# Bias stage without GpSimd work and with blocks in alternating halves, eight copies of remainder rows, an earlier k split and scatters in two places

## The chip, the cores and the metric

The kernel runs on one core of one Trainium2 chip. The metric is the device time of one execution in microseconds (us); lower is better. Engines are PE (TensorE), DVE (VectorE), ACT (ScalarE), POOL (GpSimd) and SP (SyncE, which here only issues DMAs). A name with a q at its end (SPq, POOLq) is the engine's instruction sequencer, and PEld is the load of weights into PE.

## The reference

Two layers in float32, attention and then a mixture of experts. Attention has 8 batches, 8 heads, 576 positions and 64 columns a head, and a bias that depends on the two positions alone and is made by a small MLP with 32 hidden units:

```python
pos = np.arange(S)
rel = (pos[:, None] - pos[None, :]).astype(np.float32)
x = (np.log1p(np.abs(rel)) / np.log1p(np.maximum(pos[:, None].astype(np.float32), 1.0)))[..., None]
bias = np.maximum(x @ w1 + b1, 0.0) @ w2
scores = scale * np.matmul(q, k.transpose(0, 1, 3, 2)) + bias.transpose(2, 0, 1)[None]
attn = softmax(scores)                      # rows less their maximum
y = np.matmul(attn, v)
```

The rows of y, one for each of the 4608 tokens with 512 columns, go to the experts. Each token takes the one expert of eight with the largest logit:

```python
logits = x @ w_gate + modality_bias[modality_id]
e_idx, gate_w = np.argmax(logits, axis=1), max of softmax(logits)
for e in range(E):
    mask = e_idx == e
    h = np.maximum(x[mask] @ w1[e], 0.0)            # 512 -> 1024
    out[mask] = gate_w[mask, None] * (h @ w2[e])    # 1024 -> 512
```

## The kernel before, in words

The program is one stream that Python writes in order; each engine runs its own instructions in that order, and waits where one depends on another engine or on a DMA. Nothing reorders it. There are four stages.

**Bias (0 to 75 us).** Every element of the bias is an MLP of log1p of the distance, so a hidden row is a shifted window of one table: `xTb[0]` holds the table scaled by w1 (loaded in two pieces from `c_tg`, scaled by L157), and one hidden instruction (L179, on DVE or ACT) adds a column and takes the maximum with 0 over 128 partitions (4 rows of the bias by 32 units) and 576 columns. Four of these make a block: `bias_out` (L182) multiplies them with w2 on PE, `bias_put` (L197) scales the PSUM result into one of four output buffers (in `xTb[1]`) on ACT, or on DVE for the blocks in PUT_DVE, and SP stores the output into the bias tables in SBUF. 32 blocks fill the main table `NBm`, of 128 partitions; each store writes 16 partitions, 8 heads and 576 columns. `bias_base` (L48) says which: block blk writes partitions o + 64 half and every fourth of 16 behind it, with c = blk % 4, half = blk // 4 % 2 and o = blk // 8, so that four blocks in a row write the same half of the partitions. Four further blocks, made in `bias_late` (L249) during the first pair of heads, fill `NBr`, the bias of the last 64 rows, with eight copies each (L212). ON_DVE names the blocks of which DVE makes all four hidden instructions; in the others ACT makes one.

Beside the blocks stand hooks by block (`first_steps`, L524): loads of q, k and v of the first two pairs, the split of q and k into a rounded part and the rest (`split`, L352: a cast at L356 and a subtraction at L357, both on POOL), their transposes (`prep`), and the steps of `route_setup` (L616), which makes the constants of routing (memsets, loads, the id table's fill, the modality bias `mbias` at L691) on POOL and SP, one step at each block of ROUTE.

**Attention (75 to 700 us).** There are 32 pairs of heads, four to a batch. For a pair, 576 query rows make five tiles, u = 0 to 4 (four of 128 rows, one with the remainder). ORDER (L559) is a string of letters for each u: S scores (`scores`, L406), e and f exponentials, C the compaction of remainder rows on POOL (L455), t and T transposes of the exponentials, R, a, A, b and c the product with v, 0 to 4 the transposes of q and k of pair n+1, W the swap of QT (`swap`, L391: two DMAs on SP that bring columns to the other half of the partitions), K the heads' copies, V and L loads, q the split of q of pair n+2, k the split of k of pair n+1. X, B, Z and D are routing of the batch before: X and B its arithmetic and its rows, D their store to `xg` in DRAM (L883, on SP), and Z one scatter of token ids into the expert table `tab` by an indirect DMA that POOL issues (L862). `route_next` (L887) takes the next step of a list when the list it needs has come far enough.

**First expert tiles (700 to 790 us).** `first_tiles` (L1223) puts into the last four pairs what the first tiles need: the ids, the first expert's w1 at (2, 0) and w2 at (3, 4), each a tuple of pair and u. The weights go into slots of `NBm` (`moe_early`, L898) whose bias rows are no longer needed. `tile` (L1192) works on 256 rows: `phase1` (L1144) multiplies with w1, `phase2` (L1165) with w2, where `wsplit` (L1115) splits weights into two parts by a cast on ACT (L1123, L1130) and a subtraction on DVE (L1124, L1131). For tile 0 three of w2's subtractions run on POOL. The last batch's routing runs beside tile 0 in steps (`moe_first`, L1249).

**The other tiles (790 to 1185 us)** run to the end by tables of the tokens an expert has.

## Time and profile before

| | us |
|---|---|
| median of three runs (1186.39 to 1190.75) | 1189.63 |
| the profiled execution | 1186.77 |
| its span in the trace | 1184.9 |
| PE busy in it | 1125.8 |
| DVE, ACT and POOL busy | 756.1, 727.6, 384.0 |

The mean granted clock of PE was 0.988. The span is the time from the first to the last instruction of the trace; the execution's own time is 1.9 us longer. A busy engine is one with an instruction in flight; for PE that counts matmuls that overlap. In rows of waits, `<-` inside a name separates output and inputs of an instruction, and in brackets stands how long it waited and what came last. A row by stretches has the stretch, its length, then busy us and instructions (of all engines in the order PE, PEld, DVE, ACT, POOL where five are given), the granted clock of PE as a share of full speed, the busy share of the 16 DMA engines and what they moved in GB/s.

### The profile page before, as it was taken

How to read it: one execution, taken by the hardware profiler on the slowest of the kernel's cores; microseconds unless marked ns; L12 is line 12 of the kernel's file. 1: busy time of each engine (PE TensorE's matmuls, PEld its weight loads, DVE VectorE, ACT ScalarE, POOL GpSimd, SP SyncE). 2: the span in 40 equal slices, each digit the busy share in tenths (PEclk: the TensorE clock that was granted, in tenths of full speed). 3: DMA queues.
4: the chain of work that ended last, by engine and by line, in shares of the span. 5: the costliest groups of instructions: out<-in, count | busy, mean ns of one | idle time of the engine just before them, and what ended most of it. 6: DMA issues, size and time to landing. Idle time of an engine off the chain costs nothing. (4 is left out here: it accounts for less than half of the span.)

```text
span 1184.9 us, 23097 instructions
## 1 busy us (share of the span) xinstructions
PE 1125.8 (95%) x8202; PEld 915.2 (77%) x8202; DVE 756.1 (64%) x1552; ACT 727.6 (61%) x1412; POOL 384.0 (32%) x525
## 2 busy tenths in 40 slices
PE   7976999999999999999999979999999999999997
PEld 3455777767778677777877757988999899999975
DVE  7974567556665575766757647677456645655567
ACT  5564667667777576677775745555455545544576
POOL 2303222534534434344353224622221222122121
PEclk9997999999999999999999989999999999999999
DMA  6954444564544545444454540221123314211371
GB/s 173 197 120 123 110 104 99 113 112 121 118 102 114 107 121 104 120 120 109 114 123 96 162 103 25 70 54 37 45 64 107 117 45 159 92 46 54 116 251 30
DMA packets 91312, 124.27 MB, mean 105 GB/s; under 512 B 35697, under 2 KB 60657, under 8 KB 91188
## 3 DMA queue, kind: packets, MB, share of 16 engines
q1 hardware_dynamic: 83188, 101.35, 34.9%
q0 software_dynamic: 8000, 21.35, 6.0%
q8 instruction: 68, 1.11, 0.5%
q14 instruction: 56, 0.46, 0.2%
HBM read 140.09 MB, written 19.90 MB: 135 GB/s over the span
## 5 line engine op out<-in xcount | busy, mean ns | idle before, releaser
L436 DVE CUSTOM_DVE_ANT_0 Eb<-sps,NBm 128x576 f32<-128x576 f32 x256 | 190.1, 755 | 175.3 <-PE sps L421 85.5
L450 ACT ACTIVATE Eb<-Eb,mn 128x576 f32<-128x576 f32 x288 | 221.3, 769 | 42.5 <-DVE mn L436 37.9
L421 PE MATMUL sps<-KT,QT 128*128 128x288 f32 x1152 | 221.2, 318 | 21.1 <-DMA QT<-QT 19.3
L421 PEld LDWEIGHTS sps<-KT,QT 128*128 128x128 f32 x1152 | 165.1, 190 | 26.7 <-issue 18.1
L1157 PE MATMUL p<-QT,w1hi 128*128 128x256 f32 x1152 | 163.8, 285 | 5.0 <-ACT w1hi L1130 5.0
L464 PE MATMUL eps<-idf,Eb 128*128 128x128 f32 x1024 | 158.0, 280 | 0.5 <-DVE lgs L784 0.3
L1157 PEld LDWEIGHTS p<-QT,w1hi 128*128 128x128 f32 x1152 | 150.7, 193 | 7.1 <-ACT w1hi L1130 5.9
L508 PE MATMUL xps<-eT,vraw 128*64 128x288 f32 x1024 | 153.5, 421 | 1.5 <-DVE QT L1142 1.0
L1183 POOL DMA_INDIRECT out<-mo,idt x36 | 51.9, 1440 | 290.6 <-ACT mo L1182 262.2
L464 PEld LDWEIGHTS eps<-idf,Eb 128*128 128x128 f32 x1024 | 113.6, 141 | 38.3 <-issue 28.2
L1160 DVE SCALAR_TENSOR_TENSOR hl<-p,hh 128x512 fp32r<-128x512 f32 x72 | 49.7, 690 | 138.2 <-ACT hh L1159 134.4
L455 POOL COPY rem<-Eb 128x128 f32<-128x128 f32 x128 | 37.7, 295 | 275.4 <-ACT Eb L450 268.8
L1174 PE MATMUL p<-w2lo,hh 128*128 128x512 f32 x288 | 112.9, 392 | 3.5 <-DVE w2lo L1124 2.2
L310 ACT ACTIVATE eT<-eps 128x512 f32<-128x512 f32 x192 | 111.1, 591 | 6.3 <-PE eps L464 5.5
L1124 DVE TENSOR_TENSOR w2lo<-NBm,w2hi 128x1024 fp32r<-128x1024 f32 x81 | 98.7, 1225 | 25.2 <-ACT w2hi L1123 23.6
L1174 PE MATMUL p<-w2hi,hh 128*128 128x512 f32 x288 | 114.0, 396 | 0.0
L1174 PE MATMUL p<-w2hi,hl 128*128 128x512 f32 x288 | 112.5, 391 | 0.0
L1159 ACT ACTIVATE hh<-p 128x512 fp32r<-128x512 f32 x72 | 43.0, 598 | 110.6 <-PE p L1157 101.2
L310 ACT ACTIVATE xTb<-xps 128x288 f32<-128x288 f32 x64 | 26.3, 412 | 121.5 <-PE xps L518 119.5
L1124 DVE TENSOR_TENSOR w1lo<-NBm,w1hi 128x1024 fp32r<-128x1024 f32 x84 | 97.9, 1228 | 0.0
L508 PEld LDWEIGHTS xps<-eT,vraw 128*64 128x64 f32 x1024 | 62.6, 137 | 45.7 <-issue 11.4
L1157 PE MATMUL p<-QT,w1lo 128*128 128x256 f32 x576 | 93.1, 284 | 1.0 <-DVE w1lo L1131 1.0
(227 smaller groups left out, 1991.8 us busy)
## 6 DMA issues: line engine op xcount, KB each, us to landing
NBm<-moe_w SPq DMA_DIRECT2D x24, 2048.0 KB
NBm<-moe_w SPq DMA_DIRECT2D x46, 1024.0 KB
QT<-QT SPq DMA_DIRECT2D x64, 304.0 KB
NBm<-xTb SPq DMA_DIRECT2D x32, 288.0 KB
KH<-KT SPq DMA_DIRECT2D x64, 144.0 KB
qraw<-q SPq DMA_DIRECT2D x32, 256.0 KB
kraw<-k SPq DMA_DIRECT2D x32, 256.0 KB
vraw<-v SPq DMA_DIRECT2D x32, 256.0 KB
```

Source lines behind the costliest of these rows:

```text
L310: self.nc.scalar.activation(out, ps, AF.Copy, scale=scale)
L421: nc.tensor.matmul(ps[:, half, :], q, k[:, HS * half : HS * half + HS], start=i == 0, stop=i == len(terms) - 1, skip_group_check=True,)
L436: nc.vector.tensor_tensor_reduce(out=e.rearrange("p (t w) -> p t w", t=2), in0=ps, in1=nb.rearrange("p (t w) -> p t w", t=2), scale=1.0, s ...
L450: self.nc.scalar.activation(e, e, AF.Exp, bias=mn, scale=-1.0, accum_out=sm)
L464: nc.tensor.transpose(ps[:, k, :], e[:, part, P * k : P * k + P], self.idf)
L508: nc.tensor.matmul(ps[o, :], v[:, h, k, :], self.eT[:, h, k, sl], start=k == 0, stop=False, tile_position=(0, 64 * h), skip_group_check=True,)
L1124: (lo or self.nc.vector).tensor_tensor(l, w, h.bitcast(F32), op=ALU.subtract)
L1157: nc.tensor.matmul(ps[:, a, :], w[:, c, fs], x[:, c, :], start=i == 0, stop=i == len(ops) - 1)
L1159: nc.scalar.activation(hh[:, sl, :], ps, AF.Relu)
L1160: nc.vector.scalar_tensor_tensor(hl[:, sl, :], ps, 0.0, hh[:, sl, :].bitcast(F32), op0=ALU.max, op1=ALU.subtract)
L1174: nc.tensor.matmul(ps, h[:, f, sl], m[:, f, :], start=i == 0, stop=i == len(ops) - 1)
L1183: nc.gpsimd.indirect_dma_start(out=self.out, out_offset=IndirectOffsetOnAxis(ap=ids, axis=0), in_=o, in_offset=None, bounds_check=self.n_t ...
```

## The change

The new code, part by part:

- **Blocks.** `bias_base` now takes half = blk % 2, c = blk // 2 % 4 and o = blk // 8, so that blocks in a row write different halves. The offsets of the table change with it: X0 is 115 instead of 131, and the remainder blocks have a table of their own, `tg1` (loaded at block 15, scaled by ACT at block 23), whose rows are ordered so that a block's 16 rows are neighbours. A remainder block is then stored by two copies of 16 partitions each instead of eight of 4.
- **Who does what in the bias stage.** ON_DVE has 5 blocks instead of 9, PUT_DVE 3 instead of 2. Two small loads go through ACT's queue. The splits of pairs 0 and 1 are a cast on ACT and, two blocks later, a subtraction on DVE (`early`). The load of v of pair 0 moves from block 0 to block 19.
- **Routing's set-up.** Its memsets move ahead of the bias stage, six loads stay beside the blocks (ROUTE), and the other loads, the fills of `tab` and `xg`, and the modality bias move to u-steps of pairs 1 to 3 (ROUTE_LATE), with `xrb` as their buffer.
- **ORDER.** k is split at u = 4 for pair n+2 instead of u = 0 for pair n+1. Z stands at u = 0 and u = 2 and no longer at u = 3; scatters have a list of their own, and what is left of it runs behind the last pair.
- **First expert tiles.** The slots of `NBm` are shared out differently (w1's and w2's first weights in slots 0 and 1), the load of w2 stands at (3, 0) instead of (3, 4), all of w2's subtractions are DVE's and stand ahead of the routing steps, `phase2` runs the products with the low part of w2 last, and routing's steps beside tile 0 come two later.

```diff
@@ -41,22 +41,22 @@
-X0 = 131
-TW = X0 + S4
+X0, X1 = 115, 15
+TW, TW1 = X0 + S4, X1 + S4
...
-        c, half, o = blk % 4, blk // 4 % 2, blk // 8
+        half, c, o = blk % 2, blk // 2 % 4, blk // 8
         return o + 16 * cg + 64 * half, c
-    return P + cg, blk - NMAIN
+    return P + 4 * (blk - NMAIN) + cg, 0
@@ -110,17 +112,20 @@
-    ON_POOL, ON_DVE = (), (1, 6, 11, 15, 17, 21, 24, 27, 29)
+    ON_POOL, ON_DVE = (), (1, 8, 15, 22, 29)
...
-    PUT_DVE, ON_ACT2 = (21, 34), ()
-    PREP0, SWAP0, HEADS0, QK1, SPLIT1 = (9, 10, 13, 14, 17), 20, 23, (9, 10, 11, 12, 13, 14), 17
-    ROUTE = (1, 1, 2, 4, 5, 6, 7, 8, 15, 16, 17, 20, 21, 24, 25, 26, 27, 28, 29, 29)
+    PUT_DVE, ON_ACT2 = (21, 31, 34), ()
+    SPLIT0, PREP0, SWAP0, HEADS0, QK1, SPLIT1 = (3, 5), (9, 10, 13, 14, 17), 20, 23, (9, 10, 11, 12, 13, 14), (18, 21)
+    V0, TG1 = 19, (15, 23)
+    ROUTE = (6, 7, 8, 15, 16, 18)
+
+    ROUTE_LATE = ((1, 1), (1, 2), (1, 3), (1, 4), (2, 0), (2, 1), (2, 3), (3, 0), (3, 1))
@@ -128,21 +133,23 @@
-        nc.sync.dma_start(wb[:, 0:1], io["w1"].rearrange("o m -> m o"))
         nc.sync.dma_start(cb, io["c_bias"])
-        nc.sync.dma_start(wb[:, 1:2], io["b1"].rearrange("(m o) -> m o", o=1))
+        nc.scalar.dma_start(wb[:, 0:1], io["w1"].rearrange("o m -> m o"))
         nc.sync.dma_start(wb[:, 2 : 2 + H], io["w2"])
+        nc.scalar.dma_start(wb[:, 1:2], io["b1"].rearrange("(m o) -> m o", o=1))
@@ -206,10 +213,9 @@
-            for cg in range(4):
-                for par in range(2):
-                    r0 = 64 * par + 4 * cg + c
-                    nc.sync.dma_start(self.NBr[r0 : r0 + 49 : 16, :, :], o[32 * cg + par : 32 * cg + 32 : 2, :])
+            r0 = 16 * (blk - NMAIN)
+            for par in range(2):
+                nc.sync.dma_start(self.NBr[64 * par + r0 : 64 * par + r0 + 16, :, :], o[par:P:2, :])
@@ -349,12 +354,16 @@
-    def split(self, n, part):
+    def split(self, n, part, early=False):
...
+        lo = lambda eng: eng.tensor_tensor(xs[:, :, 1, :], x, xs[:, :, 0, :].bitcast(F32), op=ALU.subtract)
+        if early:
+            self.nc.scalar.copy(xs[:, :, 0, :], x)
+            return lambda: lo(self.nc.vector)
         self.nc.gpsimd.tensor_copy(xs[:, :, 0, :], x)
-        self.nc.gpsimd.tensor_tensor(xs[:, :, 1, :], x, xs[:, :, 0, :].bitcast(F32), op=ALU.subtract)
+        lo(self.nc.gpsimd)
@@ -531,13 +540,19 @@
-        add(0, lambda: self.load_v(0))
-        add(2, lambda: self.split(0, 0))
-        add(4, lambda: self.split(0, 1))
+        add(self.V0, lambda: self.load_v(0))
+        for part in range(2):
+            early(self.SPLIT0[part], 0, part)
+        add(self.TG1[0], lambda: self.nc.sync.dma_start(self.tg1, self.io["c_tg1"]))
+        add(self.TG1[1], lambda: self.nc.scalar.activation(self.tg1, self.tg1, AF.Copy, scale=self.w1c[:, 0:1]))
@@ -556,17 +572,20 @@
-        "S R S e f k X T a t B C Z",
+        "S R S e f X T a t B C Z",
         "L D S 1 A t e S 4 f 0 C T",
         "t S W S e f b q C Z T",
-        "B S c e S T 3 2 t f C Z V",
-        "S K X X e T B X t D",
+        "B S c e S T 3 2 t f C V",
+        "S K k X X e T B X t D",
@@ -595,21 +614,25 @@
-                    elif op in "qL":
+                    elif op in "qkL":
                         if n + 2 < n_pair:
-                            self.split(n + 2, 0) if op == "q" else self.load_qk(n + 2)
+                            self.load_qk(n + 2) if op == "L" else self.split(n + 2, "qk".index(op))
...
+                    elif op == "Z":
+                        self.route_scatter()
...
+        while self.scatters:
+            self.route_scatter()
@@ -829,6 +855,8 @@
+            if b < self.B - 1:
+                self.scatters += [s_scatter(c) for c in range(5)]
@@ -883,13 +909,18 @@
+    def route_scatter(self):
+
+        if self.scatters:
+            self.scatters.pop(0)()
@@ -922,9 +953,9 @@
-        self.wst, self.ws = [w[0], w[3]], [w[1], w[2]]
-        self.xr = [slots[:, c, 1, 0:XW] for c in range(2)]
-        self.lt = slots[:, 2, 1, 0:XW]
+        self.wst, self.ws = [w[0], w[1]], [w[2], w[3]]
+        self.xr = [slots[:, c, 2, 0:XW] for c in range(2)]
+        self.lt = slots[:, 2, 2, 0:XW]
@@ -1169,7 +1200,7 @@
-            ops = [(h, m, f) for f in range(NFC) for h, m in ((hh, hi), (hl, hi), (hh, lo))]
+            ops = [(h, hi, f) for f in range(NFC) for h in (hh, hl)] + [(hh, lo, f) for f in range(NFC)]
@@ -1195,9 +1226,8 @@
         def split():
+            self.wsplit(1, next(parts))
             beside()
-            part = next(parts)
-            self.wsplit(1, part, lo=self.nc.gpsimd if t == 0 and self.K and part < 3 else None)
@@ -1235,7 +1265,7 @@
-        add(3, 4, lambda: self.load_w("first", 0, 1, self.wst[1]))
+        add(3, 0, lambda: self.load_w("first", 0, 1, self.wst[1]))
@@ -1249,7 +1279,7 @@
-        steps = iter("X,XX,BBB,,,X,BX,XB,XB,XB,B,XB,B,B,B,B,,B,B,B,B,B,,B".split(","))
+        steps = iter(",,X,XX,BBB,,X,BX,XB,XB,XB,B,XB,B,B,B,B,B,B,B,B,B,B".split(","))
```

The order of the instructions on an engine, before and after, at three places. A row has the line, the operation, the output and inputs, the shape and the number of such instructions in a row. First SP, behind the last store of the main bias table; `one` is a routing constant, `qraw` and `kraw` are raw q and k of pair 2, and the last two rows are the swap of QT for pair 1. Before:

```order
L207 DMA NBm<-xTb_95 16x8x576 x9
L907 DMA one<-c_one 1x51
L212 DMA NBr<-xTb_95 4x4x576 x32
L328 DMA qraw_856<-q 128x2x256
L334 DMA qraw_856<-q 64x64 x2
L328 DMA kraw_860<-k 128x2x256
L334 DMA kraw_860<-k 64x64 x2
L394 DMA QT_73<-QT_73 64x1216
L395 DMA QT_73<-QT_73 64x1216
```

And after, at the same place:

```order
L214 DMA NBm<-xTb_95 16x8x576 x9
L938 DMA one<-c_one 1x51
L218 DMA NBr<-xTb_95 16x4x576 x8
L333 DMA qraw_817<-q 128x2x256
L339 DMA qraw_817<-q 64x64 x2
L333 DMA kraw_821<-k 128x2x256
L339 DMA kraw_821<-k 64x64 x2
L403 DMA QT_73<-QT_73 64x1216
L404 DMA QT_73<-QT_73 64x1216
```

The eight copies of 16 partitions stand where 32 copies of 4 stood; what is behind them is in the same order.

Next POOL beside the bias, from the memset of `ones` on. Before:

```order
L631 MEMSET ones 128x128
L356 CAST qs<-qraw_147 128x9x64
L357 TENSOR_TENSOR qs<-qraw_147,qs 128x9x64
L356 CAST ks<-kraw_151 128x9x64
L357 TENSOR_TENSOR ks<-kraw_151,ks 128x9x64
L645 MEMSET wgb 128x128
L656 MEMSET Eb 128x289
L660 MEMSET Eb 1x516
L666 MEMSET Eb 128x80
L356 CAST qs<-qraw_323 128x9x64
```

And after:

```order
L650 MEMSET ones 128x128
L652 MEMSET wgb 128x128
L655 MEMSET lt_124 128x64
L657 MEMSET rec 128x40
L659 MEMSET oh 128x48
L661 MEMSET ohb 128x96
L464 COPY rem_0_791<-Eb 128x128
L464 COPY rem_1_853<-Eb 128x128
L365 CAST qs<-qraw_817 128x9x64
L361 TENSOR_TENSOR qs<-qraw_817,qs 128x9x64
```

The first rows with an input (the copies to `rem`) belong to pair 0, behind the bias; between the memsets and them POOL has nothing left to do.

Last POOL in the last pair and behind it. The copies to `rem` are the compactions of pair 31, `xrb` are the last rows of batch 6's routing on their way to `xg`, and `L1091` gathers the first tile's tokens. Before:

```order
L455 COPY rem_0_7587<-Eb 128x128
L862 DMA tab<-ids,pos_7530 36992x1
L455 COPY rem_1_7616<-Eb 128x128
L455 COPY rem_2_7644<-Eb 128x128
L862 DMA tab<-ids,pos_7530 36992x1
L455 COPY rem_3_7682<-Eb 128x128
L862 DMA tab<-ids,pos_7530 36992x1
L845 TENSOR_TENSOR xrb_89<-xrb_89,rec 128x512
L848 COPY xrb_89<-gt_7447 128x4
L845 TENSOR_TENSOR xrb_90<-xrb_90,rec 64x512
L848 COPY xrb_90<-gt_7447 64x4
L1091 DMA NBr<-xg,idt_737 128x516 x2
```

And after:

```order
L464 COPY rem_0_7570<-Eb 128x128
L890 DMA tab<-ids,pos_7508 36992x1
L464 COPY rem_1_7599<-Eb 128x128
L464 COPY rem_2_7627<-Eb 128x128
L890 DMA tab<-ids,pos_7508 36992x1
L464 COPY rem_3_7665<-Eb 128x128
L873 TENSOR_TENSOR xrb_89<-xrb_89,rec 128x512
L876 COPY xrb_89<-gt_7425 128x4
L873 TENSOR_TENSOR xrb_90<-xrb_90,rec 64x512
L876 COPY xrb_90<-gt_7425 64x4
L1122 DMA NBr<-xg,idt_724 128x516 x2
L890 DMA tab<-ids,pos_7508 36992x1 x2
```

The third scatter of the pair stood ahead of the last rows and now stands behind the gather, with the one that followed it before.

More of the change, by code (lines that the diff above doesn't have):

```diff
@@ L41 @@
 NBLK = S4 // 4
-X0 = 131
-TW = X0 + S4
+X0, X1 = 115, 15
+TW, TW1 = X0 + S4, X1 + S4
 def bias_base(blk, cg):
     if blk < NMAIN:
-        c, half, o = blk % 4, blk // 4 % 2, blk // 8
+        half, c, o = blk % 2, blk // 2 % 4, blk // 8
         return o + 16 * cg + 64 * half, c
-    return P + cg, blk - NMAIN
+    return P + 4 * (blk - NMAIN) + cg, 0
 def bias_rows(blk, cg):
     s, c = bias_base(blk, cg)
-    return [4 * (s + 4 * g) + c for g in range(4)]
+    return [4 * (s + 4 * g) + c if blk < NMAIN else 4 * s + g for g in range(4)]
 def n_tiles(n_tok):
@@ L170, in bias_hidden @@
         s, c = bias_base(blk, cg)
-        win = self.tg[:, 3 - c : 7 - c, X0 - s : TW - s]
+        win = self.tg[:, 3 - c : 7 - c, X0 - s : TW - s] if blk < NMAIN else self.tg1[:, :, X1 + P - s : TW1 + P - s]
         c = self.shift[:, 4 * blk + cg : 4 * blk + cg + 1]
@@ L532, in first_steps, with early @@
         evac = {}
+        def early(blk, n, part):
+            add(blk, lambda: evac.update({(n, part): self.split(n, part, early=True)}))
+            add(blk + 2, lambda: evac.pop((n, part))())
         def pe(k):
@@ L549, in first_steps @@
                 add(blk, lambda: next(loads, None))
-            add(self.SPLIT1, lambda: self.split(1, 0))
+            for part in range(2):
+                early(self.SPLIT1[part], 1, part)
         for blk in self.ROUTE:
@@ L569, in attention @@
         tail = self.first_tiles() if self.K else {}
+        for at in self.ROUTE_LATE:
+            tail.setdefault(at, []).append(lambda: next(self.route, None))
         for u, k in self.LATE:
@@ L652, in route_setup @@
             yield
[L654 to L657 removed]
+        x0, x1 = self.xrb
+        zr = x1[0:1, 0:XW]
+        nc.gpsimd.memset(zr, 0.0)
+        m2 = x0[:, 0 : 2 * NC].bitcast(I32).rearrange("p (b c w) -> p b c w", b=B, c=5)
+        nc.gpsimd.memset(m2, 0)
         yield
[L659 to L660 removed]
         nc.sync.dma_start(self.xg[self.n_tok : self.n_tok + 1, :], zr)
[L662 removed]
         mid = io["moe_modality_id"].bitcast(I32)
[L665 to L666 removed]
         nc.sync.dma_start(
@@ L674, in route_setup @@
         )
-        mb = E8[:, 5, n_fill : n_fill + 2 * E].rearrange("p (a e) -> p a e", a=2)
+        yield
+        n_fill = (E * self.n_tab + SS) // P
+        fill = x1[:, 0:n_fill].bitcast(I32)
+        nc.gpsimd.memset(fill, self.n_tok)
+        tri = x1[:, n_fill : n_fill + P]
+        nc.sync.dma_start(tri, io["c_tri"])
+        yield
+        mb = x1[:, n_fill + P : n_fill + P + 2 * E].rearrange("p (a e) -> p a e", a=2)
         nc.sync.dma_start(
@@ L680, in route_setup @@
         yield
-        for _ in range(4):
-            yield
-        mf = E8[:, 6, 2 * NC : 3 * NC]
-        nc.gpsimd.tensor_copy(self.tri, E8[:, 5, S - P : S])
+        nc.sync.dma_start(self.tab.rearrange("(p w) o -> p (w o)", p=P), fill)
+        yield
+        self.tri = cp.tile([P, P], BF16, name="tri")
+        nc.gpsimd.tensor_copy(self.tri, tri)
+        mf, m1 = x0[:, 2 * NC : 3 * NC], x0[:, 3 * NC : 4 * NC]
         nc.gpsimd.tensor_copy(mf, m2.rearrange("p b c w -> p (b c) w")[:, :, 0])
+        nc.gpsimd.tensor_scalar(m1, mf, -1.0, 1.0, op0=ALU.mult, op1=ALU.add)
         self.mbias = cp.tile([P, NC, E], F32, name="mbias")
-        t0 = E8[:, 6, 4 * NC : 12 * NC].rearrange("p (n e) -> p n e", e=E)
-        m1 = E8[:, 6, 3 * NC : 4 * NC]
-        nc.gpsimd.tensor_scalar(m1, mf, -1.0, 1.0, op0=ALU.mult, op1=ALU.add)
+        yield
+        t0 = x0[:, 4 * NC : 12 * NC].rearrange("p (n e) -> p n e", e=E)
         for a, (dst, mk) in enumerate(((t0, m1), (self.mbias, mf))):
@@ L873, in route_steps @@
         ot = [(0, s_recip), (4, s_top), (4, s_onehot), (4, s_gate), (5, s_pos)]
-        scatters = [(5, s_scatter(c)) for c in range(5)]
         if b == self.B - 1:
-            ot += scatters + [(6, f) for f in self.last_tables()]
-            scatters = []
-        return [[px, 0], [ot, 0], [scatters, 0]]
+            ot += [(5, s_scatter(c)) for c in range(5)] + [(6, f) for f in self.last_tables()]
+        return [[px, 0], [ot, 0]]
     def route_store(self):
@@ L891, in route_next @@
         need, f = bg[kind][0][bg[kind][1]]
-        if bg[0 if kind == 1 else 1][1] < need:
+        if bg[1 - kind][1] < need:
             return None
@@ L1408, in build @@
                     self.attn_early(ast, rst)
+                    self.route = self.route_setup(rp)
+                    next(self.route)
                     self.bias_setup()
-                    hooks = self.first_steps(self.route_setup(rp))
+                    hooks = self.first_steps(self.route)
                     self.bias_table(hooks)
```

59 lines of the change are left out of this document (25 added, 34 removed).

## The prediction

> **What bounds the kernel now.** I read the busy shares first, then the stretches by stage, then the waits in each. One row of the page says where time can be won:
> ```profile
> PE 1125.8 (95%) x8202; PEld 915.2 (77%) x8202; DVE 756.1 (64%) x1552; ACT 727.6 (61%) x1412; POOL 384.0 (32%) x525
> ```
> PE is busy for all but 59 us, so a change that leaves PE's work alone can win those 59 us, time in which PE runs at a lowered clock, and the bias stage, where PE's "busy" is only overlap of small matmuls that another engine feeds. The stretches (us; PE busy and instructions; granted clock; DMA share; GB/s):
> ```profile
> 66.40:84.10 17.70, 15.25 (x147) 1.00 0.42 100
> 84.10:98.00 13.90, 0.01 (x1) 0.65 0.50 137
> 98.00:130.00 32.00, 31.95 (x234) 0.94 0.43 107
> 130.00:660.00 530.00, 518.21 (x4065) 1.00 0.49 111
> 700.40:705.40 5.00, 0.02 (x1) 0.73 0.46 96
> 705.40:735.00 29.60, 26.66 (x163) 0.93 0.03 9
> 735.00:1100.00 365.00, 363.45 (x2390) 1.00 0.23 74
> 1100.00:1184.90 84.90, 75.88 (x406) 0.97 0.41 135
> ```
> Two stretches have no PE work: 13.9 us in pair 0 and 5.0 us between attention and the experts. The clock falls in both and is still low behind them: 0.94 over 32.0 us is 1.9 us lost, 0.93 over 29.6 us is 2.1 us. In 130 to 660 us 11.8 us are idle. From 735 to 1100 us PE waits 1.6 us, and the 9 idle us behind 1100 lie in code that the diff doesn't reach. So the gain is in five places, which I take in order of time.
>
> **Start, 0.8 us gained (0.3 to 1.0).** Four small loads stand ahead of the shifted table in SP's queue; two move to ACT's.
> ```profile
> 1.68 0.42 SPq L140 DMA_DIRECT2D xrb<-b  x1
> 2.15 0.42 SPq L141 DMA_DIRECT2D xrb<-w  x1
> ```
> Issues stand 0.47 us apart, so the table's issue moves up by two of them, 0.9 us, less what a later small load might hold back. ACT is idle then.
>
> **Bias stage, 5.0 us gained (-1 to 8).** All engines until 66.4 us (PE, PEld, DVE, ACT, POOL), then the hidden-layer instructions of L179 on DVE alone, by stretches with and without POOL work:
> ```profile
> 0.00:66.40 66.40, 56.96 (x532) 26.44 (x532) 59.32 (x121) 40.23 (x58) 16.91 (x30) 1.00 0.84 187
> 7.30:15.00 7.70, 7.67 (x11) 1.00 0.46 127
> 46.90:52.60 5.70, 5.05 (x6) 1.00 0.95 201
> 52.60:66.40 13.80, 13.80 (x33) 1.00 1.05 201
> 50.91 1.50 POOL L357 TENSOR_TENSOR ks<-kraw,ks 128x576 fp32r<-128x576 f32 x1
> L202 DVE TENSOR_SCALAR xTb<-bps,xrb x1: 805/805/805, 51.1 to 51.1; 128x576 f32<-128x576 f32 x1
> ```
> DVE is busy from its first table on and sets the pace. Where POOL rests, 33 hidden instructions take 13.80 us, 0.42 us each. In two stretches in which POOL splits q and k (L357's row is in the second) 11 take 7.67 us and 6 take 5.05. Over 0.42 us each, that is 3.1 + 2.5 = 5.6 us which DVE loses to POOL; POOL's other work here adds, so I take 6.5. The change takes POOL's work out of this stage, so they go. Nine blocks with four hidden instructions on DVE become five: 4 x 0.42 = 1.7 us more. Against it stand one more eviction, 0.8 us by L202's row, and four subtractions for the splits. By the row
> ```profile
> L1124 DVE TENSOR_TENSOR w2lo<-NBm,w2hi 128x1024 fp32r<-128x1024 f32 x81 | 98.7, 1225 | 25.2 <-ACT w2hi L1123 23.6
> ```
> 1024 columns take 1.23 us; a split has 576, so 0.7 us (an estimate in proportion), 2.8 us for four. DVE's net gain is 6.5 + 1.7 - 0.8 - 2.8 = 4.6 us. ACT takes four hidden instructions, four casts and the small table's scaling, some 6 us on 40.23 us busy of 66.4: covered.
>
> But the stores of this stage fill the DMA engines:
> ```profile
> 25.00:70.00 45.00, 1.00 1.00 203
> 58.00:58.50 0.50, 0.50 (x2) 1.00 1.20 257
> 61.50:62.00 0.50, 0.50 (x2) 1.00 1.04 198
> ```
> Their share is 1.00 over 45 us at 203 GB/s (the last two columns; ahead of the clock stand the hidden instructions in the two short rows), 9.14 MB. The small table (0.33 MB) and v of pair 0 (0.29) move in, the id table's fill (0.15) moves out: 9.6 MB. At 203 GB/s that takes 47.3 us, and nothing is won, nor at the next step. Now four stores in a row write one half of the partitions; the half microsecond at 257 GB/s beside one at 198 suggests that engines on different halves don't hinder each other. With every second store in the other half I take 240 GB/s, nearer to the peak: 40.0 us, 5.0 us less than 45, about what DVE gains. That is the term, with the shorter wait of the last evictions for free output buffers inside it. The bounds: 203 GB/s (-1), and both limits at their best plus that wait (8).
>
> The Trainium skill speaks against this edit: "SBUF — State Buffer", section "Can I just issue two DMAs to hit both halves?", says that two concurrent transfers on different halves run only 6% faster than one, because they serialize. By that the rate would be 215 GB/s, the stores would take 44.7 us, and this term would be 0.3 us instead of 5.0. The peak speaks against the rule, though it is short.
>
> **The rows behind the main table, 14.0 us gained (11 to 18).**
> ```profile
> 70.94 18.41 SPq L212 DMA_DIRECT2D NBr<-xTb  x32
> 75.37 0.30 ACT L204 ACTIVATE xTb<-xps,xrb 128x64 f32<-128x64 f32 x1
> 77.22 0.88 DVE L314 TENSOR_SCALAR QT<-xps 128x128 fp32r<-128x128 f32 x2
> 91.33 0.76 DVE L436 CUSTOM_DVE_ANT_0 Eb<-sps,NBr 128x576 f32<-128x576 f32 x1 [8.35 <-DMA NBr<-xTb]
> 92.97 0.54 SPq L394 DMA_DIRECT2D QT<-QT  x1
> 98.05 0.82 PE L421 MATMUL sps<-KT,QT 128*128 128x288 f32 x2 [13.93 <-DMA QT<-QT]
> ```
> The 32 copies hold SP for 18.41 us, 0.58 each. Behind them stand six loads of q and k (89.40 to 92.97 us by the same queue), then the swap of QT, on which PE's next scores wait. Eight copies take 4.6 us, but the last two can't start before the last eviction ends at 75.67: SP is free at 76.9 instead of 89.4 us, the loads end at 80.4, and the swap (its source ready at 78.1) is issued there. It took 5.1 us from 92.97 to 98.05, so PE goes on at 85.5 to 86.5 us, where it stood still from 84.1: 12.0 of 13.9 us go, and QT's swap is still what is late. A gap of 2 us doesn't lower the clock in this trace (from 130 to 660 us it stays at 1.00 beside waits of up to 2.5, next part), so 2.0 us of clock come back. If eight copies of four times the size land late, DVE waits at 91.33's place for NBr instead; 9 us of stall would go.
>
> **Attention, 4.0 us gained (0 to 8).** What PE waits for from 130 to 680 us (total, times, longest), and one cause:
> ```profile
> PE sps L421 <- DMA QT<-QT: 5.4, 4, 2.5
> PE xps L375 <- POOL ks L357: 2.9, 2, 1.9
> PE xps L492 <- POOL rem L455: 0.4, 1, 0.4
> 230.44 0.98 POOL L862 DMA_INDIRECT tab<-ids,pos  x1 [5.04 <-DMA QD<-QT]
> ```
> POOL's scatters block its queue (5.04 us here) with the routed rows and the k split behind them; rows late on POOL make SP late with stores, loads and the swap. Splitting k four steps earlier takes the 2.9 us away; scatters at two places with a half pair between them have landed mostly when the next is due. I take 2.9 + 0.4 and 0.7 of the swap's 5.4: its issue also waits for DVE. The route's set-up moves into pairs 1 to 3; POOL is idle for over half of each pair and those transfers are under 0.2 MB each, so nothing is added. Bounds: all 8.7 us, and none, where the rows queue behind the k split instead.
>
> **From attention to the experts, 10.0 us gained (5 to 11.5).**
> ```profile
> 683.41 2.59 SPq L1085 DMA_DIRECT2D NBm<-moe_w  x2
> 694.23 0.98 POOL L862 DMA_INDIRECT tab<-ids,pos  x1 [7.19 <-DMA tab<-ids,pos]
> 696.44 1.59 SPq L883 DMA_DIRECT2D xg<-xrb  x2
> 698.86 0.41 ACT L310 ACTIVATE xTb<-xps 128x288 f32<-128x288 f32 x1 [2.82 <-PE xps L518]
> 704.28 1.99 ACT L1130 CAST w1hi<-NBm 128x1024 fp32r<-128x1024 f32 x2 [5.01 <-DMA xg<-xrb]
> ```
> 2 MB of weights are issued at 683.4; the scatter that waits behind them holds POOL until 694.23, the last rows follow on POOL, their store at 696.44 lands at 704.28, and only then is the buffer's memory free for the experts' weights, on which PE waits 5.0 us. The load moves four steps ahead, to where its slot of the bias table is free since pair 29, and the third scatter moves behind the rows: their store goes out near 691 us and lands before the last ACT eviction (698.86 + 0.41). The cast (half of 1.99 us) then ends at 700.3, when PE gets there: 5.0 us go, and 2.0 us of clock. In the first tiles
> ```profile
> 715.47 5.75 POOL L1124 TENSOR_TENSOR w2lo<-NBm,w2hi 128x1024 fp32r<-128x1024 f32 x2
> 716.35 2.61 DVE L1131 TENSOR_TENSOR w1lo<-NBm,w1hi 128x1024 fp32r<-128x1024 f32 x1
> 725.69 0.50 PE L1174 MATMUL p<-w2lo,hh 128*128 128x512 f32 x1 [1.29 <-POOL w2lo L1124]
> 779.15 0.50 PE L1174 MATMUL p<-w2lo,hh 128*128 128x512 f32 x1 [1.55 <-DVE w2lo L1124]
> ```
> three subtractions on POOL take 2.9 us each and double DVE's own beside them (2.61 for 1.23). On DVE they cost 3 x 1.23 = 3.7 us and the doubling goes, with routing work two steps later. PE idles 2.9 us in this stretch and 1.55 at 779; with all low-part matmuls of w2 at the end of a pass, up to 14 matmuls later, I take 3.0 of these 4.5.
>
> **Sum:** 0.8 + 5.0 + 14.0 + 4.0 + 10.0 = 33.8 us. The profiled execution took 1186.8 us, 2.9 less than the median of the runs, within their spread of 4.4. 1186.8 - 33.8 = 1153.0.
>
> **The rivals.** (1) The store rate stays at 203 GB/s: the bias term goes, 1158; the skill's 6% gives the same within 0.3. For it: share 1.00 over 45 us; against it: the peak. (2) The copies are traded for another wait in pair 0 (NBr's landing, or the swap behind the loads): 5 us of that term stay, 1158. (3) The weights' memory waits for something else, say the scatters that now stand behind the rows: 5 us and the clock stay, 1160. (4) The edit doesn't do what it says in the large places, since the queues still hold their work back elsewhere: within 6 us of 1187; the order printed above speaks against it. (5) Slower: k's split, 1.50 us of POOL for its subtraction (row above) and a cast, stands ahead of the routed rows and the next pair's compaction in every pair. If PE waited for it in each of 30 pairs, 1.1 us per pair would cancel the gain and 1.33 would be slower by 0.5%; the full 1.50 us give 1153 + 45 = 1198. Against it: PE waits 0.4 us for compactions in 550 us.
>
> **How the numbers follow.** Forecast 0.60; rivals (1) 0.15, (2) 0.10, (3) 0.08, (4) 0.04, (5) 0.03. All terms at their ends give 1187 - 46 to 1187 - 15, which seldom meet; 1142 to 1170 holds the forecast's range and rivals (1) to (3), singly and together (1153 + 5 + 5 + 7 = 1170). A measurement of this kernel tells about 0.5%, 6 us, from no change. Faster by more: 0.93; within it: 0.04; slower: 0.03.
>
> **What would show it.** The table's hidden instructions at 0.42 us throughout and the last main-table store some 5 us earlier, with a rate near 240; eight copies and a gap under 3 us before pair 1's scores; no PE wait for the k split; the w1 cast behind the last ACT eviction and not behind a store, the clock at 1.00 there. It would be wrong above all if the store rate did not rise, or if pair 0 found another late transfer.

## The result, and the profile after

| | us | ratio to before |
|---|---|---|
| before, median of 4 runs (1186.39 to 1190.75) | 1189.03 | |
| changed, median of 4 runs (1153.10 to 1160.33) | 1159.05 | 0.974 (95%: 0.970 to 0.978) |
| profiled executions, before and after | 1186.77, 1160.33 | |
| forecast | 1153.0 (1142 to 1170) | |

The change wins 30.0 us by the medians and 26.4 us between the two profiled executions, where 33.8 were forecast. In the experiments below the kernel before took more, 1195.7 to 1198.4 us in the median, and the changed kernel as long as here (1158.56 us in run 8), so that by run 8 the change wins 37.6 us; no profile shows where the kernel before loses the 7 us more. The same instructions of PE, in the two timelines, show where the 26.4 us come from. First before (start, duration, engine, line, operation, shapes, count, idle time ahead of it): the first bias products, the first scores of pair 0, the last scores of pair 31, and the first product with w1.

```profile
9.33 1.96 PE L188 MATMUL bps<-eT,xrb 128*32 128x512 f32 x8 [4.72 <-ACT eT L177]
70.84 1.32 PE L421 MATMUL sps<-KT,QT 128*128 128x288 f32 x8
...
685.63 0.80 PE L421 MATMUL sps<-KT,QT 128*128 128x288 f32 x4
...
705.38 2.08 PE L1157 MATMUL p<-QT,w1hi 128*128 128x256 f32 x8 [5.01 <-ACT w1hi L1130]
```

And after, with the scores behind the swap of pair 0 as the third row (98.05 before, in the prediction):

```profile
8.33 3.03 PE L195 MATMUL bps<-eT,xrb 128*32 128x512 f32 x19 [4.13 <-ACT eT L184]
67.89 1.32 PE L430 MATMUL sps<-KT,QT 128*128 128x288 f32 x8
83.54 0.50 PE L430 MATMUL sps<-KT,QT 128*128 128x288 f32 x2 [2.39 <-DMA QT<-QT]
...
661.84 0.80 PE L430 MATMUL sps<-KT,QT 128*128 128x288 f32 x4
...
681.16 1.22 PE L1188 MATMUL p<-QT,w1hi 128*128 128x256 f32 x8
```

The lead over before is 1.0 us at the first products, 2.95 at the first scores, 14.5 behind the swap, 23.8 at the last scores, 24.2 at the first product with w1 and 26.5 at the end (1184.9 less 1158.4). So the steps won 1.0 (forecast 0.8), 2.0 (5.0), 11.6 (14.0), 9.3 (4.0) and 2.7 (10.0). PE after, by stretches (us; PE busy and instructions; clock; DMA share; GB/s):

```profile
83.60:115.00 31.40, 31.40 (x232) 0.95 0.50 117
115.00:640.00 525.00, 520.01 (x4092) 1.00 0.49 114
664.00:676.00 12.00, 9.65 (x49) 0.72 0.50 73
708.00:1073.00 365.00, 362.85 (x2377) 1.00 0.23 74
```

Attention idles 5.0 us in 525 where it idled 11.8 in 530. The 5.0 us without PE work ahead of the experts are gone, but a new hole at 664 to 676 us has 2.35 us idle at a clock of 0.72, and 2.15 us are idle in the last row where 1.55 were.

### The profile page after: what moved, and what is told of

Its sections match the earlier page's. It is cut to its first block, busy times and chain, and to the rows that moved or that the text cites. A ratio compares the mean times of both kernels' runs of the same rounds, so it can differ in the third digit from the quotient of the medians.

```text
span 1158.4 us, 23054 instructions
## 1 busy us (share of the span) xinstructions
PE 1121.5 (97%) x8202; PEld 912.4 (79%) x8202; DVE 748.6 (65%) x1556; ACT 731.8 (63%) x1420; POOL 361.0 (31%) x514
## 3 DMA queue, kind: packets, MB, share of 16 engines
q8 instruction: 68, 1.11, 0.5%
## 5 line engine op out<-in xcount | busy, mean ns | idle before, releaser
L1214 POOL DMA_INDIRECT out<-mo,idt x36 | 48.0, 1333 | 298.5 <-ACT mo L1213 262.4
L1155 DVE TENSOR_TENSOR w2lo<-NBm,w2hi 128x1024 fp32r<-128x1024 f32 x84 | 102.3, 1224 | 24.8 <-ACT w2hi L1154 18.7
L1154 ACT CAST w2hi<-NBm 128x1024 fp32r<-128x1024 f32 x84 | 86.8, 1040 | 0.7 <-PEq L1318 0.7
```

The lines of the kernel that those rows point to most:

```text
L1154: self.nc.scalar.copy(h, w)
L1155: self.nc.vector.tensor_tensor(l, w, h.bitcast(F32), op=ALU.subtract)
L1214: nc.gpsimd.indirect_dma_start(out=self.out, out_offset=IndirectOffsetOnAxis(ap=ids, axis=0), in_=o, in_offset=None, bounds_check=self.n_t ...
```

## Experiments

All edits are to the changed kernel, except in the ninth. Ratios are to the kernel before in runs on the same chip, with 95% intervals. The eighth, e8_again, is the changed kernel without an edit on the chip of runs 5 to 7: 1158.56 us, 0.969 (0.967 to 0.971). Time differences at a place compare its PE instruction with that of the first profile of the changed kernel, where no other run is named.

**1. The number of copies** (e1_copies32)

```diff
-                nc.sync.dma_start(self.NBr[64 * par + r0 : 64 * par + r0 + 16, :, :], o[par:P:2, :])
+                for cg in range(4):
+                    r = 64 * par + r0 + 4 * cg
+                    nc.sync.dma_start(self.NBr[r : r + 4, :, :], o[32 * cg + par : 32 * cg + 32 : 2, :])
```

> The changed kernel, but each of its eight copies of remainder rows is issued as four of 4 partitions: 32 copies of the same data. Theory (SP's issue time is what counts): the copies hold SP for about 18 us instead of 6.8, the swap of QT in pair 0 lands some 11 us later, PE's gap before its next scores grows from 2.4 to about 13.5 us and the lowered clock behind it from 3.4 to about 13.7 us, so the time rises by 14 us or more. Rival (the small table's row order and the blocks in halves let the rows land early, the number of copies matters little): the gap stays below 4 us and the time within 2 us.

Measured: 1173.28 us, ratio 0.982 (0.976 to 0.987). Timelines of SP and PE, then SP in the changed kernel:

```profile
66.27 21.75 SPq L220 DMA_DIRECT2D NBr<-xTb  x32
...
96.72 0.82 PE L432 MATMUL sps<-KT,QT 128*128 128x288 f32 x2 [17.16 <-DMA QT<-QT]
```
```profile
67.33 6.80 SPq L218 DMA_DIRECT2D NBr<-xTb  x8
```

32 copies of the same data hold SP 15 us longer, and PE waits 14.8 us longer for the swap behind them. The theory holds; the scores behind stand 14.8 us later relative to the pair's first.

**2. Blocks in halves** (e2_same_half)

```diff
-        half, c, o = blk % 2, blk // 2 % 4, blk // 8
+        c, half, o = blk % 4, blk // 4 % 2, blk // 8
```

> The changed kernel with the old order of blocks: four stores in a row write the same half of the partitions. Theory (halves matter for the rate of the stores): from 25 to 60 us the rate falls from about 225 to about 203 GB/s, ACT's evictions wait for stores longer, the last store of the main table is issued 4 to 6 us later (64 us now) and the time rises by 3 to 6 us. Rival (halves do not matter, as a 6% rule says; the rate rose since DVE fed the stores faster): the rate stays at 215 to 230 GB/s and the time within 1.5 us.

Measured: 1160.49 us, 0.971 (0.966 to 0.976). The same stretch of the bias stage, in the kernel before, the changed one and this one:

```profile
25.00:65.00 40.00, 39.33 (x372) 1.00 1.00 203
```
```profile
25.00:65.00 40.00, 35.57 (x370) 0.94 0.96 224
```
```profile
25.00:65.00 40.00, 35.16 (x354) 0.96 1.05 208
```

SP is through the main table's stores 2.7 us later (67.3 against 64.5 us) and pair 0's first scores stand 2.8 us later. So the halves are worth 224 against 208 GB/s, 8%, and 2.8 us at this place; 4 to 6 us were expected. The median is 1.4 us above the changed kernel's first and 1.9 above its second, where 3 to 6 us were expected: less than the runs can tell. Against the profile of run 8, which like this one has a clock of 1.00 from 664 to 676 us, the end stands 2.5 us later.

**3. Splits on POOL** (e3_pool_split)

```diff
-            self.nc.scalar.copy(xs[:, :, 0, :], x)
-            return lambda: lo(self.nc.vector)
+            self.nc.gpsimd.tensor_copy(xs[:, :, 0, :], x)
+            return lambda: lo(self.nc.gpsimd)
```

> The changed kernel with the four splits of pairs 0 and 1 on POOL again, at the same blocks. Theory (the stores set the end of the stage, DVE has slack behind 50 us): hidden instructions beside the splits take 0.7 to 1.1 us instead of 0.43, but the last store of the main table is issued within 1.5 us of 64 us, and the time rises by 0 to 2 us. Rival (DVE is still the bound, as the prediction's working had it): the last store is issued 3 to 6 us later and the time rises by 3 to 6 us.

Measured: 1157.96 us, 0.968 (0.963 to 0.973). The bias products that stood at 40 us stand 2.9 us later, those at 54 to 61 us only 1.1 to 1.5; the last store of the main table is issued 0.8 later (64.8 against 64.0 us), and the first scores stand 0.8 earlier. DVE does lose time beside POOL, but the stores set the end of the stage. In the changed kernel (groups by line of DVE, then timelines of ACT and DVE):

```profile
L186 DVE TENSOR_SCALAR eT<-xTb,xrb 128x576 f32<-128x576 f32 x61 | 28.3, 515 | 0.5 <-PE bps L195 0.4
...
L361 DVE TENSOR_TENSOR qs<-qraw,qs 128x576 fp32r<-128x576 f32 x2 | 1.5, 756 | 0.1
```
```profile
51.63 0.74 ACT L211 ACTIVATE xTb<-bps,xrb 128x576 f32<-128x576 f32 x1 [2.46 <-DMA NBm<-xTb]
```
```profile
63.10 0.82 DVE L209 TENSOR_SCALAR xTb<-bps,xrb 128x576 f32<-128x576 f32 x1 [4.04 <-PE bps L195]
```

A hidden instruction of the largest group takes 515 ns in the mean; before, the same group had 589:

```profile
L179 DVE TENSOR_SCALAR eT<-xTb,xrb 128x576 f32<-128x576 f32 x63 | 34.3, 589 | 0.0
```

DVE is through its table at 59.1 us (66.9 before), ACT waits for stores to free its output buffers, and DVE then stands idle for 4.04 us. The theory holds.

That the first scores come earlier although the stores end later has a second cause, which the profile of run 12 shows (its edit lies in the experts, its bias stage is the changed kernel's). PE from 60 to 68 us, in the kernel before, the changed one and run 12, and then the first scores in run 12:

```profile
60.00:68.00 8.00, 6.50 (x72) 1.00 1.05 208
```
```profile
60.00:68.00 8.00, 6.25 (x56) 0.57 0.67 179
```
```profile
60.00:68.00 8.00, 6.02 (x76) 1.00 0.75 202
```
```profile
66.06 1.33 PE L430 MATMUL sps<-KT,QT 128*128 128x288 f32 x8
```

SP is through the main table's stores at 64.5 us in the changed kernel and at 64.2 in run 12, but the first scores stand at 67.89 and 66.06 us. PE waits for DVE near 64 us in both (1.11 and 1.21 us); in the changed kernel its clock is lowered there, in run 12 it isn't, and that costs the first scores some 1.5 us. In run 3's own profile the clock is 1.00 at that place.

**4. The swap ahead of the loads** (e4_swap_first)

```diff
+                            elif n > 0:
+                                self.load_qk(n + 2)
...
-"W": lambda: self.swap(n + 1),
+"W": lambda: (self.swap(n + 1), self.load_qk(n + 2) if n == 0 else None),
```

> The changed kernel with the six loads of q and k of pair 2 behind the swap of QT in pair 0, not ahead of it. Theory (the swap behind these loads is what PE waits for at 81 us, 2.4 us, and the half clock for 3.4 us behind it is caused by this gap): the swap is issued near 75 us instead of 78.5, the gap falls under 0.5 us, no half clock follows, and the time falls by 3 to 4.5 us. Rival (the swap waits for DMA engines that are busy with the remainder rows, or POOL's split of q of pair 2 holds up the compaction): the gap stays over 1.5 us or an equal wait for the compacted rows takes its place, and the time is within 1 us.

Measured: 1160.73 us, 0.971 (0.964 to 0.978). PE's waits from 78 to 92 us:

```profile
83.06 0.51 PE L430 MATMUL sps<-KT,QT 128*128 128x288 f32 x2 [1.03 <-DMA QT<-QT]
86.47 0.71 PE L501 MATMUL xps<-idf,rem 128*128 128x128 f32 x2 [2.68 <-POOL rem L464]
```

The rival's second half holds: the gap shrinks from 2.39 to 1.03 us, but POOL waits 7.20 us for q of pair 2, whose split stands ahead of the compaction (4.34 in the changed kernel), and PE for POOL. The swap behind the loads is a cause of the gap, and moving the loads only trades it for another.

**5. The k split in its old place** (e5_k_old)

```diff
-        "S R S e f X T a t B C Z",
+        "S R S e f k X T a t B C Z",
...
-        "S K k X X e T B X t D",
+        "S K X X e T B X t D",
...
+                                {"k": lambda: self.split(n + 1, 1), ...
```

> The changed kernel with k split at u = 0 for the next pair again (pair 1's too), scatters as in the change. Theory (the earlier k split is what took the waits of 2.9 us for it away): PE waits for the split of k one to three times behind scatters, 2 to 4 us in all from 120 to 690 us, with a half clock behind some, and the time rises by 2 to 5 us. Rival (the scatters' new places did it, and k's place is worth nothing): no wait for k's split over 0.5 us, time within 1.5 us.

**6. A third scatter at u = 3** (e6_scatter3)

```diff
-        "B S c e S T 3 2 t f C V",
+        "B S c e S T 3 2 t f C Z V",
```

> The changed kernel with a third scatter at u = 3 of each pair, k split as in the change. Theory (two scatters a tile apart make POOL wait for the landing of the first with rows and splits behind it): POOL's waits for the scatter's landing before a scatter return, PE waits for swaps or rows 2 to 4 us more from 120 to 690 us, and the time rises by 2 to 5 us. Rival (the gain in attention is the k split's alone or chance): PE's waits in that stretch within 1.5 us of those of the changed kernel, time within 1.5 us.

**9. The scatters' part alone, on the kernel before** (e9_before_2z)

```diff
-        "B S c e S T 3 2 t f C Z V",
+        "B S c e S T 3 2 t f C V",
...
+                    elif op == "Z":
+                        self.route_scatter()
...
+        while self.scatters:
+            self.route_scatter()
...
+            if b < self.B - 1:
+                self.scatters += [s_scatter(c) for c in range(5)]
```

> The kernel before with the scatters' part of the change alone: their own list, places at u = 0 and u = 2, the rest behind the last pair; k's split stays at u = 0. Theory (the third scatter's place is what cost time in attention): POOL's idle time ahead of the scatters falls from 47 to some 10 us from 130 to 660 us, PE's waits for swaps and for k's split in attention fall from 8.3 to under 3 us, and the stretch from pair 1 to the last pair becomes 6 to 10 us shorter. Rival (k's place is needed too): the waits for k's split (2.9 us) stay and the stretch is at most 5 us shorter.

Measured: 5 took 1156.34 us, 0.967 (0.965 to 0.968); 6 took 1190.07 us, 0.996 (0.992 to 1.000); 9 took 1179.45 us, 0.987 (0.982 to 0.991). The scatters on POOL from 130 to 660 us (busy, mean ns, idle time ahead of them and what ended it), in the kernel before, the changed one, and runs 5, 6 and 9:

```profile
L862 POOL DMA_INDIRECT tab<-ids,pos x30 | 30.1, 1002 | 47.4 <-DMA tab<-ids,pos 33.0 <-DMA QD<-QT 9.1 <-DVE mn L436 3.2
```
```profile
L890 POOL DMA_INDIRECT tab<-ids,pos x31 | 31.2, 1006 | 10.4 <-DMA tab<-ids,pos 6.3 <-issue 3.9
```
```profile
L889 POOL DMA_INDIRECT tab<-ids,pos x31 | 31.3, 1011 | 8.8 <-DMA tab<-ids,pos 4.6 <-issue 3.6
```
```profile
L890 POOL DMA_INDIRECT tab<-ids,pos x30 | 30.1, 1003 | 41.5 <-DMA tab<-ids,pos 16.9 <-DMA KH<-KT 11.5 <-DMA vrem<-v 5.5
```
```profile
L868 POOL DMA_INDIRECT tab<-ids,pos x30 | 30.0, 1001 | 11.2 <-DMA tab<-ids,pos 7.3 <-issue 3.3 <-DVE mn L436 0.2
```

It is the third scatter of a pair that makes POOL wait, in the kernel before mostly (33.0 of 47.4 us) for the one before it to land, and not k's place: with k back at u = 0 PE has no wait for its split (5 and 9). The theory of run 5 falls, and with it that part of the prediction. The third scatter (6) costs far more than the 2 to 5 us that were expected: 31.5 us against run 8 on the same chip, more than the change wins in the first runs. So run 6's theory has the mechanism, but not the size. With k at u = 4 and the third scatter, PE's waits from 120 to 690 us are

```profile
PE sps L430 <- DMA QT<-QT: 14.2, 6, 4.8
...
PE xps L384 <- POOL ks L361: 1.6, 1, 1.6
```

and attention is 21.5 us longer than in the changed kernel; the wait for the cast of w1 is back as well, with 6.98 us (none in the changed kernel). This is the fastest of its five executions. Its timelines of POOL and PE show the chain:

```profile
216.69 0.98 POOL L890 DMA_INDIRECT tab<-ids,pos  x1 [6.96 <-DMA KH<-KT]
218.44 1.40 POOL L361 TENSOR_TENSOR ks<-kraw,ks 128x576 fp32r<-128x576 f32 x1
219.81 1.04 POOL L873 TENSOR_TENSOR xrb<-xrb,rec 128x512 f32<-128x512 f32 x1
```
```profile
236.41 0.80 PE L430 MATMUL sps<-KT,QT 128*128 128x288 f32 x2 [4.80 <-DMA QT<-QT]
```

POOL stands 6.96 us ahead of a scatter, splits k, and only then scales the routed rows (the row names a copy of KH; the scatter before had landed 0.2 us earlier, at 216.4 us); their store stands ahead of loads and swap in SP's queue, and PE waits 4.80 us for the swap. Run 9 wins 5.9 us from pair 1 to the last pair, just under what was expected. At the first product with w1 it leads the profile of the kernel before by 11.0 us, so the wait of 5.01 us for the cast went with the scatters as well; but 5.5 us are lost again in tile 0, where PE waits for DVE's subtractions of w1 (total, times, longest):

```profile
PE p L1165 <- DVE w1lo L1139: 6.2, 2, 5.4
```

By the medians run 9 wins 16.2 us (1195.66 to 1179.45), by the profiles 7.9: the profile of the kernel before is from the first runs, and its time is 8.9 us under the median on this chip.

**7. The load of w2 in its old place** (e7_w2_late)

```diff
-        add(3, 0, lambda: self.load_w("first", 0, 1, self.wst[1]))
+        add(3, 4, lambda: self.load_w("first", 0, 1, self.wst[1]))
```

> The changed kernel with the first load of w2 at (3, 4) again. Theory (the rows' store behind 2 MB of weights is what the experts' memory waits for): the wait of PE for the first cast of w1 returns with 3 to 5 us and the half clock behind it, the wait for the rows' eviction near 665 us (1.3 us) goes, and PE's first product with w1 stands 2 to 6 us later than without. Rival (the third scatter's place did it): PE's first product with w1 has no wait over 1 us and the time is within 1.5 us.

Measured: 1157.31 us, 0.967 (0.964 to 0.970). PE's first product with w1 stands at 681.09 us (681.16 in the changed kernel) without a wait. The rival holds, as runs 6 and 9 show from the other side: the third scatter returns the wait although w2 loads early, and without it the wait goes although w2 loads late. One part of the theory comes true: the wait for the rows' eviction near 665 us is gone. SP in the changed kernel, then in run 7 (`moe_w` is the load of w2, `xg` the rows' store; the last of three joined stores here is issued at 657.53 us):

```profile
650.89 1.32 SPq L1116 DMA_DIRECT2D NBm<-moe_w  x2
653.34 16.34 SPq L909 DMA_DIRECT2D xg<-xrb  x3
```
```profile
651.67 6.18 SPq L909 DMA_DIRECT2D xg<-xrb  x3
658.75 1.01 SPq L1116 DMA_DIRECT2D NBm<-moe_w  x2
```

With 2 MB of weights ahead of it the store lands 12.2 us after its issue (653.34 to 665.56 us), with the weights behind it 2.0 us (657.53 to 659.56).

**8. No edit** (e8_again)

> The changed kernel once more, without an edit, on the chip of these runs. Theory (a transfer that lands some 5 us late by chance makes the waits near 665 us and the swaps' waits): the wait of ACT for a row buffer near 665 us and the half clock of 6.8 us behind it are gone or smaller, other waits for swaps stand in other pairs, and the span differs by up to 5 us. Rival (these waits belong to the order of instructions): the same waits in the same places within 0.3 us.

The hole at 664 us in this profile:

```profile
664.00:676.00 12.00, 10.48 (x78) 1.00 0.55 76
```

78 matmuls in the 12 us against 49, at a clock of 1.00 against 0.72, worth 4.4 us between the last scores and the first product with w1. In the first profile ACT and POOL wait for the rows' store, and PE for ACT:

```profile
665.66 0.59 ACT L315 ACTIVATE xrb<-xps 64x512 f32<-64x512 f32 x1 [1.63 <-DMA xg<-xrb]
...
665.63 0.99 POOL L890 DMA_INDIRECT tab<-ids,pos  x1 [6.79 <-DMA xg<-xrb]
...
666.40 0.91 PE L501 MATMUL xps<-idf,rem 128*128 128x128 f32 x4 [1.30 <-ACT xrb L315]
```

And in run 8, where it was issued at 653.31 us:

```profile
664.56 0.99 POOL L890 DMA_INDIRECT tab<-ids,pos  x1 [5.26 <-DMA xg<-xrb]
```

Both guesses hold in part. The late landing belongs to the order of instructions: here too POOL waits for the store, until 664.56 us, 11.2 us after its issue, and in the other profiles with the weights ahead of it the store takes 11.2 to 12.1 us. What differs from profile to profile is the last 1 us, and whether PE's short waits are followed by a lowered clock: PE waits 0 to 0.8 us for ACT at this place in the other profiles, 1.30 in the first, and only there and in run 1 the clock falls. The wait near 728 us, 2.2 us, is in this profile too and belongs to the order.

**10. A version with two further edits** (e12_both)

```diff
+                            if op == "L" and n > 0:
+                                self.load_qk(n + 2)
+                            elif op == "q" and n > 0:
+                                self.split(n + 2, 0)
+                            elif op == "k":
+                                if n == 0:
+                                    self.split(n + 2, 0)
+                                self.split(n + 2, 1)
...
+"W": lambda: (self.swap(n + 1), self.load_qk(n + 2) if n == 0 else None),
...
-        steps = iter(",,X,XX,BBB,,X,BX,XB,XB,XB,B,XB,B,B,B,B,B,B,B,B,B".split(","))
+        steps = iter(",,X,XX,BBB,,X,BX,XB,XB,B,XB,XB,B,B,B,B,B,B,B,B,B".split(","))
```

> The changed kernel with two edits: in pair 0 the loads of q and k of pair 2 stand behind the swap and the split of that q stands at u = 4; and one step of routing's rows beside tile 1 moves from behind the preparation of the next tile's tokens to the end of that tile's second product. Theory (both gaps are queue order): the gap at 81 us (2.4 us) falls under 1.2 us with no wait for compacted rows in its place, the wait of 2.2 us near 728 us goes with its half clock of 3.4 us, and the time falls by 4 to 7 us. Rival (the first gap is the flight time of the swap, the second only moves to the next step): at most 2 us.

Measured: 1153.12 us (median of 6), 0.964 (0.961 to 0.968), 5.4 us under the changed kernel's second median; the intervals of the two just touch. Waits of PE in the changed kernel at the second place, DVE beside it, and then what is left in this version at the first:

```profile
728.64 0.66 PE L866 MATMUL xps<-idf,xTb 128*128 128x128 f32 x4 [2.15 <-DVE QT L1173]
```
```profile
722.80 5.18 DVE L1155 TENSOR_TENSOR w1lo<-NBm,w1hi 128x1024 fp32r<-128x1024 f32 x4 [0.20 <-ACT w1hi L1154]
727.91 1.27 DVE L1173 TENSOR_TENSOR QT<-xps,QT 128x512 fp32r<-128x512 f32 x2
```
```profile
83.58 0.51 PE L430 MATMUL sps<-KT,QT 128*128 128x288 f32 x2 [0.94 <-DMA QT<-QT]
```

No wait stands at the second place any more, and the clock is 1.00 from 84 to 740 us. The step at 728 us needed a PSUM bank that DVE frees only behind four subtractions: the changed kernel had moved it there, and that cost 2.15 us of waiting and, in its two profiles, 1.6 us of clock behind it (0.95 over 32 us). The run has both edits, so no run tells what each is worth in the whole time.

**11. Tile 0's subtractions on POOL** (e13_pool_lo)

```diff
-            self.wsplit(1, next(parts))
+            part = next(parts)
+            self.wsplit(1, part, lo=self.nc.gpsimd if t == 0 and self.K and part < 3 else None)
             beside()
```

> The changed kernel with three of the four subtractions for w2 of tile 0 on POOL again. Theory (POOL doubles DVE's time beside it and w2's low parts come late): PE waits 1 to 2 us more in the first tile, for w1's or w2's low part, and its first product with w2's low part stands 1 to 3 us later. Rival (with the products of w2's low part last, POOL's lateness is hidden): within 0.5 us.

**12. The old order of products in phase2** (e14_phase2)

```diff
-            ops = [(h, hi, f) for f in range(NFC) for h in (hh, hl)] + [(hh, lo, f) for f in range(NFC)]
+            ops = [(h, m, f) for f in range(NFC) for h, m in ((hh, hi), (hl, hi), (hh, lo))]
```

> The changed kernel with the old order of products in phase2 (for each part of the hidden rows both products with the high part of w2, then the one with its low part). Theory (the waits for w2's low part, 1.29 us in tile 0 and 1.55 us at the end of the second tile before, went through the new order): PE waits 1 to 3 us for w2's low parts in the first three tiles, with perhaps a half clock behind, and the time rises by 1 to 4 us. Rival (they went since DVE does all of w2's subtractions, ahead of routing's steps): no wait over 0.5 us, time within 1 us.

Measured: 1158.48 us, 0.968 (0.964 to 0.973), and 1159.63 us, 0.967 (0.963 to 0.971): neither moves the whole time by what the runs can tell. In the profile of 11 PE waits for the low part of w2:

```profile
PE p L1205 <- POOL w2lo L1155: 1.1, 1, 1.1
```

and is 2.0 us later than in 8 by the second tile. In that of 12 there is no such wait, and the first three tiles take as long as in 8 to within 0.5 us. So the move to DVE took the waits away, and the order of products is worth nothing that shows.

## Why the prediction was right, point by point

- **Sum and sign.** The time lies in the range and 6 us above the forecast, the likeliest case. That the sum came so near is in part luck: in the first profile three terms were too large by 12.7 us together and one too small by 5.3. The same five steps in three profiles with the same code up to the experts (run 12 differs only in `phase2`), each against the one profile of the kernel before:

| us won | forecast | first profile | run 8 | run 12 |
|---|---|---|---|---|
| start | 0.8 | 1.0 | 0.5 | 1.1 |
| bias stage | 5.0 | 2.0 | 1.7 | 3.7 |
| the rows behind | 14.0 | 11.6 | 11.2 | 11.1 |
| attention | 4.0 | 9.3 | 9.9 | 5.5 |
| attention to experts, to the end | 10.0 | 2.7 | 5.2 | 4.4 |

Only the start and the rows behind are steady; a single profile doesn't measure the others better than to 2 to 4 us.

- **Start.** 0.5 to 1.1 us against 0.8: right.
- **Bias stage.** 1.7 to 3.7 us against 5.0. DVE gained more than worked out: 0.42 us for a hidden instruction, 0.75 us for a split where 0.7 was estimated, and it is through its table 7.8 us earlier. The last store of the main table is issued 4.5 us earlier (64.0 against 68.5 us), or 3.5 without the start's gain. What fell short was the rate, as the prediction feared: 240 GB/s was taken, 224 came. At 224 the same sum, 9.6 MB, gives 42.9 us and a term of 2.1. That this meets the first profile's 2.0 is chance: run 12 wins 3.7 with a rate of 225, and the first profile loses some 1.5 of that to the clock of 0.57 from 60 to 68 us (run 3), a loss that the prediction put at nothing. The Trainium skill's 6% ("SBUF — State Buffer", "Can I just issue two DMAs to hit both halves?") is near what run 2 shows, 8%, though the page speaks of two concurrent DMAs and here stores follow one another on one queue. The half microsecond at 257 GB/s was a peak and no rate. The rule was the better guide to the size, though not to the sum: run 2 is at 208 GB/s with the old order where the kernel before had 203.
- **The rows behind.** 11.6 us against 14.0, the mechanism shown by run 1. SP was free at 74.1 us, earlier than forecast by about what start and bias stage had won, and PE waited 2.39 us where 1.4 to 2.4 follow from the forecast. The step that failed is "a gap of 2 us doesn't lower the clock": behind this gap the clock was 0.95 for 31.4 us, 1.6 us lost, where the 1.9 before were to come back. The 1.00 on which that step rested was a mean over 530 us. Behind a wait of 1.69 us at 633.33 us the kernel before shows

```profile
633.00:641.00 8.00, 7.65 (x47) 0.79 0.11 34
```

- **Attention.** 9.3 us against 4.0, and 5.5 to 9.9 by the profile. The cause was named half rightly: POOL's scatters. The working gave 2.9 us to k's place, which is worth nothing (runs 5 and 9), and only 0.7 of 5.4 to the swaps. In the first profile PE waits 1.3 us for swaps, in run 7's 4.8. Some 5.9 us are the scatters' alone (run 9); the rest is not settled.
- **From attention to the experts.** 2.7 us against 10.0, in three parts. The wait of 5.0 us went as forecast, but by the scatter's place and not by the load's (6, 7, 9). The load's new place has a price that the prediction didn't count: it puts 2 MB ahead of the rows' store, which then lands 11 to 12 us after its issue (7, 8), so late that in the first profile PE waits for it and loses 4.4 us with the clock behind. And routing's later steps put a new wait of 2.15 us in tile 1, with a lowered clock behind it in the first profile: the order shown ahead of the prediction did not reach that place.
- **Rivals.** (1) came true in part: the rate rose to 224 and not to 240 GB/s. (2) came true in part: the swap behind the loads. (5) had the right mechanism in the wrong company: in run 6 k's split stands ahead of the late routed rows, and attention is 21.5 us longer, but only because a third scatter makes POOL late first. How much of it is k's place no run shows, since none has three scatters and k's old place in the changed kernel.

## What to carry to other kernels

An instruction that waits for its predecessor's transfer, like these scatters, blocks all that its queue holds behind it: space such instructions so far apart that the last has landed, and price an edit to that queue together with its neighbours (the third scatter costs 16.2 us in the kernel before, by run 9, and 31.5 us in the changed kernel, by run 6). A load of 2 MB that is issued early stands in front of all that its queue issues next. When two limits lie close together, as DVE and the stores here, the term is the smaller of the two gains; a rate is taken from a long stretch, not from its peaks. For a step that is moved "two later", ask what holds its buffers there. A clock of 1.00 over a long stretch can hide a lowered one, so take it behind each wait.
